# Batches 0 and 1 by head pair with a TensorE table for ALiBi and mask, later q and k transposed by DMA, and a fixed order on SyncE and GpSimd

## The chip, the cores and the metric

One core of one Trainium2 chip. The metric is the device time of one execution in microseconds (us); a kernel is given by the median of its runs. On one core an execution is called fast or slow by its distance from the fastest of the same kernel (over 1.5% is slow). A ratio between two kernels is the mean time of the fast runs of one over that of the other of the same rounds on the same chip, with a 95% interval, so it is not quite the ratio of the medians quoted beside it.

## The reference

```python
# q, k, v: (8 batches, 8 heads, 576, 64) fp32
scores = (q @ k.T) / sqrt(64)
mask   = (rel >= 0) & (rel < 128)              # rel = query - key: causal window of 128
scores = where(mask, scores - slope[h] * |rel|, -1e9)
attn   = softmax(scores) @ v
x      = heads joined: (4608 tokens, 512)
h      = x @ w_in                               # 512 -> 2048
out    = (h * sigmoid(beta * h)) @ w_out        # 2048 -> 512
```

## The kernel before

Per batch: 128-row blocks of q, k, v are loaded by SyncE (256 B rows, eight heads side by side), cast to bf16 by GpSimd, and q, k transposed by TensorE. Scores of one head pair fill a PSUM tile of two banks; four exponentials per tile carry the ALiBi bias, a multiply applies the mask. Tokens go through the two MLP layers in nine groups of 512. A "quad" is four 512-column matmuls: one hidden-layer tile (`HS`), or a quarter of an output tile (`OS`). While group g's hidden layer is computed, group g-1's output quads and the next tokens' attention are woven in. The order of TensorE's instructions is fixed by the program, the order of the other engines is chosen when it is built. Names in the profiles: `tps` is a PSUM tile of transposed q, k and `qkT` its copy in SBUF; `sps` (later `SS`, `OO`) holds scores, `pt` their exponentials, "PV" is the product of `pt` with v; `XT` is the transposed attention output that the MLP reads; `hps`, `sig` and `gT` are a hidden-layer tile, its tanh and the product of the two; `osb` is an output tile on its way to memory.

```python
    psum_h = ...tile_pool(name="psum_h", bufs=2, PSUM)
    psum_o = ...tile_pool(name="psum_o", bufs=2, PSUM)     # output tiles: two separate tiles of one bank
    psum_s = ...tile_pool(name="psum_s", bufs=1, PSUM)
    psum_t = ...tile_pool(name="psum_t", bufs=2, PSUM)
    # ... cut ...
    def T(b, sb):                                          # q, k of one 128-row block
        tps = psum_t.tile([P, 2, NP, P], BF16, name="tps", tag="t")
        for i in range(2):
            for p in range(NP):
                nc.tensor.transpose(out=tps[:, i, p, :], in_=src[:, i, 2*p:2*p+2, :]..., identity=ident[:])
        nc.vector.tensor_copy(out=QK[b % 2][:, :, :, P*sb : P*sb+rows], in_=tps[:, :, :, 0:rows])
    # ... cut ...
    def OS(g, i, n):
        if n == 0:
            opss[g, i] = psum_o.tile([P, DM], F32, name="ops", tag="ops")
        # ... four matmuls; after the fourth quad ScalarE copies the tile out (osb) and SyncE stores it
```

The softmax here doesn't subtract the row's maximum and nothing guards it: scores larger than these inputs give would overflow.

## Time and profile before

| | before |
|---|---|
| median | 374.81 us |
| first hidden-layer matmul | 42.44 us |
| TensorE busy | 338.5 us (90% of the span) |
| VectorE, ScalarE, GpSimd busy | 224.2, 214.4, 84.4 us |

Two rows of the page's slices, each digit the tenths of one fortieth of the span: TensorE's busy share and its granted clock.

```profile
PE   2367687788999999999999999999999999999995
PEclk9999999899999999999999999999999999999999
```

TensorE is short of work for the first quarter and full after it. In the list of groups (busy us, mean ns of one; then idle time before them and what ended it) two lines matter for what follows: the copy of transposed q and k into place, and the output matmuls.

```profile
L176 DVE COPY qkT<-tps 128x1024 bf16<-128x1024 bf16 x32 | 22.1, 690 | 19.6 <-PE tps L171 19.5
...
L283 PE MATMUL ops<-W,gT 128*128 128x512 bf16 x576 | 144.9, 379 | 0.0
```

The copy of 1024 columns takes 690 ns, and the 576 output matmuls never wait for anything.

### The profile page before, as it was taken

How to read it: one execution, taken by the hardware profiler on the slowest of the kernel's cores; microseconds unless marked ns; L12 is line 12 of the kernel's file. 1: busy time of each engine (PE TensorE's matmuls, PEld its weight loads, DVE VectorE, ACT ScalarE, POOL GpSimd, SP SyncE). 2: the span in 40 equal slices, each digit the busy share in tenths (PEclk: the TensorE clock that was granted, in tenths of full speed). 3: DMA queues.
4: the chain of work that ended last, by engine and by line, in shares of the span. 5: the costliest groups of instructions: out<-in, count | busy, mean ns of one | idle time of the engine just before them, and what ended most of it. 6: DMA issues, size and time to landing. Idle time of an engine off the chain costs nothing.

```text
span 374.6 us, 6713 instructions
## 1 busy us (share of the span) xinstructions
PE 338.5 (90%) x2529; PEld 172.7 (46%) x2529; DVE 224.2 (60%) x473; ACT 214.4 (57%) x437; POOL 84.4 (23%) x151
## 2 busy tenths in 40 slices
PE   2367687788999999999999999999999999999995
PEld 1145334434454455445454545454545445544442
DVE  3266467777665677665666776776767755533400
ACT  1453359375745875585846694668566854445421
POOL 7570703453122213112033303320100000000000
PEclk9999999899999999999999999999999999999999
DMA  9999999999297898954138440000000010001012
GB/s 166 209 206 202 193 195 214 192 216 180 76 214 159 159 186 170 205 126 107 50 96 187 109 104 31 28 30 29 30 28 30 30 57 29 29 29 58 28 56 86
DMA packets 121985, 42.40 MB, mean 113 GB/s; under 512 B 113232, under 2 KB 117344, under 8 KB 121952
## 3 DMA queue, kind: packets, MB, share of 16 engines
q1 hardware_dynamic: 117728, 37.77, 47.9%
q0 software_dynamic: 4224, 4.19, 6.7%
q8 instruction: 20, 0.33, 0.4%
q14 instruction: 13, 0.11, 0.1%
HBM read 36.71 MB, written 9.44 MB: 123 GB/s over the span
## 4 chain that ended last, share of the span: by engine, by line
PE 80%; DMA 6%; DVE 4%; ACT 4%; SPq 4%; issue 1%; POOL 0%; ACTq 0%
PE ops L283 34%; PE hps L267 32%; PE sps L197 4%; DMA fst<-in_k_dram 4%; PE tps L171 4%; SPq L83 4%; ACT pt L207 3%; PE xt L249 2%; PE pv L233 2%; DVE gT L273 2%; PE pv L229 2%; DMA fst<-in_v_dram 1%; ACT sig L272 1%; DVE pt L211 1%; DVE qkT L176 1%
## 5 line engine op out<-in xcount | busy, mean ns | idle before, releaser
L272 ACT ACTIVATE sig<-hps,beta_h 128x512 bf16<-128x512 f32 x144 | 99.5, 692 | 98.4 <-PE hps L267 87.4
L267 PE MATMUL hps<-XT,W 128*128 128x512 bf16 x576 | 150.7, 385 | 3.6 <-DVE gT L273 3.0
L283 PE MATMUL ops<-W,gT 128*128 128x512 bf16 x576 | 144.9, 379 | 0.0
L273 DVE SCALAR_TENSOR_TENSOR gT<-sig,hps 128x512 bf16<-128x512 bf16 x144 | 98.3, 683 | 53.0 <-ACT sig L272 52.4
L207 ACT ACTIVATE pt<-sps,bias 128x256 bf16<-128x256 f32 (+2 forms) x256 | 100.4, 480 | 34.9 <-PE sps L197 34.6
L267 PEld LDWEIGHTS <-W 128*128 128x128 bf16 x576 | 51.1, 98 | 56.5 <-issue 10.9
L283 PEld LDWEIGHTS <-gT 128*128 128x128 bf16 x576 | 51.3, 98 | 52.2 <-issue 1.7
L211 DVE TENSOR_TENSOR pt<-pt,mask 128x1024 bf16<-128x1024 bf16 x64 | 46.1, 720 | 21.2 <-ACT pt L207 20.0
L96 POOL CAST bst<-fst 128x512 bf16<-128x512 f32 (+1 forms) x40 | 24.6, 615 | 108.8 <-issue 78.7
L197 PE MATMUL sps<-qkT 64*128 64x256 bf16 (+2 forms) x320 | 28.3, 271 | 14.1 <-ACT pt L207 13.1
L104 POOL CAST vs<-fst 128x512 bf16<-128x512 f32 (+1 forms) x40 | 26.1, 659 | 65.0 <-PE pv L233 38.1
L176 DVE COPY qkT<-tps 128x1024 bf16<-128x1024 bf16 (+1 forms) x40 | 25.5, 637 | 21.5 <-PE tps L171 21.3
L171 PE MATMUL tps<-ident,bst 128*128 128x128 bf16 x320 | 28.8, 240 | 7.8 <-POOL bst L96 4.3
L239 DVE TENSOR_TENSOR xn<-pv,zs 128x256 bf16<-128x256 f32 (+1 forms) x80 | 33.7, 422 | 2.6
L289 ACT ACTIVATE osb<-ops 128x512 f32<-128x512 f32 x36 | 21.6, 601 | 20.8 <-PE ops L283 20.8
L233 PE MATMUL pv<-vs,pt 128*128 128x65 bf16 x320 | 31.0, 200 | 2.5 <-DVE xn L239 1.5
L171 PEld LDWEIGHTS <-bst 128*128 128x128 bf16 x320 | 23.5, 107 | 17.3 <-POOL bst L96 4.9
L197 PEld LDWEIGHTS <-qkT 64*128 64x128 bf16 x320 | 12.4, 97 | 38.2 <-issue 35.1
L233 PEld LDWEIGHTS <-pt 128*128 128x128 bf16 x320 | 23.6, 102 | 13.7 <-issue 1.8
L97 POOL CAST bst<-fst 128x512 bf16<-128x512 f32 (+1 forms) x40 | 25.3, 634 | 9.3 <-DMA fst<-in_k_dram 9.2
L229 PE MATMUL pv<-vs,pt 128*128 128x65 bf16 x256 | 25.8, 200 | 1.8 <-DVE qkT L176 1.2
L229 PEld LDWEIGHTS <-pt 128*128 128x128 bf16 x256 | 21.3, 102 | 8.3 <-DVE xn L239 1.3
(26 smaller groups left out, 74.3 us busy)
## 6 DMA issues: line engine op xcount, KB each, us to landing
out_dram<-osb SPq DMA_DIRECT2D x36, 256.0 KB, 2.0
fst<-in_q_dram SPq DMA_DIRECT2D x32, 256.0 KB, 4.8
fst<-in_k_dram SPq DMA_DIRECT2D x32, 256.0 KB, 4.8
fst<-in_v_dram SPq DMA_DIRECT2D x32, 256.0 KB, 5.0
W<-in_moe_w_in_dram POOLq DMA_DIRECT2D x4, 512.0 KB, 11.5
W<-in_moe_w_out_dram POOLq DMA_DIRECT2D x4, 512.0 KB, 12.6
fst<-in_q_dram SPq DMA_DIRECT2D x8, 128.0 KB, 4.2
fst<-in_k_dram SPq DMA_DIRECT2D x8, 128.0 KB, 4.2
```

The lines of the kernel that those rows point to most:

```text
L171: nc.tensor.transpose(out=tps[:, i, p, :], in_=src[:, i, 2 * p : 2 * p + 2, :].rearrange("r h d -> r (h d)"), identity=ident[:],)
L176: nc.vector.tensor_copy(out=QK[b % 2][:, :, :, P * sb : P * sb + rows], in_=tps[:, :, :, 0:rows])
L197: nc.tensor.matmul(o, lhsT=qk[64 * e : 64 * e + 64, 1, p, P * kb : P * kb + P], rhs=qk[64 * e : 64 * e + 64, 0, p, P * kb : P * kb + nq], ...
L207: nc.scalar.activation(out=pt[:, e, cols], in_=sps[:, e, cols], func=ACTF.Exp, scale=qscale, bias=bias[:, half, h : h + 1],)
L211: nc.vector.tensor_tensor(out=pt[:], in0=pt[:], in1=masks[m][:], op=ALU.mult)
L229: nc.tensor.matmul(pv[:, hl, 0 : D + 1], lhsT=weights(b, qb - 1, h, 1), rhs=vs[:, qb - 1, h, 0 : D + 1], start=True, stop=False,)
L233: nc.tensor.matmul(pv[:, hl, 0 : D + 1], lhsT=weights(b, qb, h, 0), rhs=vs[:, qb, h, 0 : D + 1], start=qb == 0, stop=True,)
L239: nc.vector.tensor_tensor(out=xn[0:nq, 4 * g : 4 * g + 4, :], in0=pv[0:nq, :, 0:D], in1=zs[0:nq].broadcast_to([nq, 4, D]), op=ALU.mult,)
L267: nc.tensor.matmul(hps[:], lhsT=W1[:, c, bass.ts(j, P)], rhs=XT[:, c, c0 : c0 + TOKG], start=(c == 0), stop=(c == NDM - 1),)
L272: nc.scalar.activation(out=sig[:], in_=hps[:], func=ACTF.Tanh, scale=beta_h[:, j : j + 1])
L273: nc.vector.scalar_tensor_tensor(out=gts[g][:, j, :], in0=sig[:], scalar=1.0, in1=hps[:], op0=ALU.add, op1=ALU.mult)
L283: nc.tensor.matmul(ops_[:], lhsT=gT[:, j, i * P : i * P + P], rhs=W2[:, j, :], start=(j == 0), stop=(j == NFF - 1),)
```

## The change

The intent: start the MLP sooner. For batches 0 and 1, q and k come one head pair at a time with four tokens, 1 KB, in one row per partition; TensorE first writes a table of ALiBi and mask into the score tile and adds the scores to it, so that one exponential per tile is enough. For batches 2 to 7, transposing DMAs take the q and k transposes off TensorE. SyncE's and GpSimd's order is now written out, and output stores go to GpSimd. The core of the diff:

```diff
+    def get_pair(what, b, p):                       # 4 tokens of one head = 1 KB in a row
+        return nc.sync.dma_start(out=f[:],
+            in_=src[b, 2*p : 2*p+2, 0:FULL, :].rearrange("h (r c) d -> r h (c d)", c=4))
+    def TP(b, p):
+        ... 8 x nc.tensor.transpose(out=tps[:, i, c], in_=src[:, i, c], identity=ident[:])
+        nc.vector.tensor_copy(
+            out=QK[b % 2][:, :, p, 0:FULL].rearrange("d i (r c) -> d i c r", c=4), in_=tps[:])
+    SS = psum_c.tile([P, 2, 512], F32, name="SS")
+    OO = psum_c.tile([P, 2, 512], F32, name="OO")
-    psum_o = ...tile_pool(name="psum_o", bufs=2, PSUM)
-    psum_s = ...tile_pool(name="psum_s", bufs=1, PSUM)
+    def SP_(b, vis, p):
+        sps = SS if vis == "A" else OO
+        ... two table matmuls (384 or 512 columns, start=True), then the scores on top (start=False)
+        nc.scalar.activation(out=pt[:, :, 0:w], in_=sps[:, :, 0:w], func=ACTF.Exp, scale=qscale)
+    def DT(b, sb):                                  # batches 2 to 7
+        nc.sync.dma_start(out=QK[b % 2][...], in_=src[...], transpose=True)
     def OS(g, i, n):
-        if n == 0:
-            opss[g, i] = psum_o.tile([P, DM], F32, name="ops", tag="ops")
-        ops_ = opss[g, i]
+        ops_ = OO[:, i % 2, :]
+    def constants_late():
+        ... 16 x nc.vector.tensor_copy(out=tablet[:, e, a, p], in_=table[:, 2*p+e, a, 0:64]), 5 memsets
+    with tc.manual_schedule(engines={ENG.PE, ENG.SP, ENG.Pool}):
+        ... batch 0, then hidden layer of group 0 with batch 1 woven in
+        # group 1: 8 hidden quads, then hidden and output quads in turn
+        # groups 2 to 8: two hidden quads to one output quad of the group before, then 8 of their own
 # ... cut: tails of 64 rows, constants, the old order ...
```

From the last group's first hidden-layer quad on, 40 quads remain instead of 48.

## The prediction

> **What bounds the kernel now.** I read the page first (busy shares, slices), then the busy time of each engine in three stretches, then the chain of waits, then TensorE's timeline in a full stretch. The stretches cut the kernel in three; the columns are length, then busy time and instructions of TensorE (PE), its weight loads, VectorE, ScalarE and GpSimd, then the granted clock, the DMA share and GB/s:
>
> ```profile
> 0.00:42.40 42.40, 21.71 (x197) 14.73 (x198) 20.64 (x64) 14.82 (x36) 23.25 (x52) 1.00 1.17 197
> 42.40:95.00 52.60, 41.00 (x323) 21.09 (x322) 36.84 (x74) 33.35 (x71) 22.75 (x37) 0.97 1.13 197
> 95.00:371.50 276.50, 275.80 (x2012) 136.86 (x2010) 166.74 (x336) 166.22 (x331) 38.39 (x64) 1.00 0.35 85
> ```
>
> From 95 us to the end TensorE never rests; there only less TensorE work helps. Before 95 us the DMA engines are full (share above 1) at 197 GB/s and TensorE is short of work. The chain of waits (start, length, what) says what the first MLP matmul waits for:
>
> ```profile
> 22.39 16.48 DMA fst<-in_k_dram
> 38.87 0.05 issue
> 38.92 0.62 POOL bst L97
> 39.55 0.05 issue
> 39.59 0.62 PE tps L171 x4
> 40.22 0.02 issue
> 40.24 0.70 DVE qkT L176
> 40.94 0.04 issue
> 40.98 0.40 PE sps L197 x2
> 41.38 0.56 PE xt L249 x4
> 41.93 0.02 issue
> 41.96 0.44 DVE XT L254
> 42.40 0.04 issue
> 42.44 1.88 PE hps L267 x4
> ```
>
> A k block (of batch 1, whose transposes TensorE meets in its queue before the last transposes of group 0) takes 16.48 us to land among W1 and the other loads; the MLP starts at 42.44 us. And TensorE where it is full; a start minus the next start is the true cost, since durations overlap:
>
> ```profile
> 128.32 1.03 PE L267 MATMUL hps<-XT,W 128*128 128x512 bf16 x4
> 129.19 0.61 PE L171 MATMUL tps<-ident,bst 128*128 128x128 bf16 x8
> 129.63 1.03 PE L283 MATMUL ops<-W,gT 128*128 128x512 bf16 x4
> 130.50 0.29 PE L233 MATMUL pv<-vs,pt 128*128 128x65 bf16 x4
> 130.63 1.02 PE L267 MATMUL hps<-XT,W 128*128 128x512 bf16 x4
> ```
>
> So four MLP matmuls cost 0.87 us (128.32 to 129.19; 0.864 in the mean), eight q/k transposes 0.44 (to 129.63), four PV matmuls 0.13. In the same way of reading, the four score matmuls of a pair took 0.32 (121.26 to 121.58), eight PV matmuls 0.24 (122.46 to 122.70), four output transposes 0.22 (124.86 to 125.08).
>
> **What the Trainium skill says.**
> 1. "TensorE: Matmul & The Clock Gate", Back-to-back issue gap: warm, about N/2.4 + 2.5 ns. The trace agrees: 216 ns at N = 512 (0.864/4) and 55 ns at N = 128 (0.44/8). I price the new 384- and 512-column table matmuls so.
> 2. "DMA: Bandwidth & Descriptors", Why small descriptors are slow: a fixed cost per packet, so 256 B rows waste the engines. The trace agrees in kind: 110,000-odd packets below 512 B, and full engines at only 197 GB/s.
> 3. The same page, Latency and other measured facts: 261 GB/s for one transposing DMA. Against it "VectorE: DVE Perf Modes", The three transpose paths: 1309 ns for one 128x128 block. No transposing DMA is in this trace; this is my largest unknown.
> 4. "SBUF — State Buffer", Door 1 trap: DMAs issued by GpSimd can starve for descriptors while VectorE holds the shared port. The output stores go there. In this trace the four W1 DMAs from GpSimd issue in 3.14 us and nothing shows the trap.
>
> **The change, part by part.**
> *TensorE work, before.* MLP 288 quads x 0.864 = 248.8. Transposes of q, k: 40 x 0.44 = 17.6. Scores: 64 x about 0.32 = 20.7. PV: 8 batches x (0.26 + 8 x 0.24) = 17.4. Output transposes 40 x 0.22 = 8.8. Sum 313 us. About 7 of it is done before 42.4 (batch 0), so 306 remain for the 329 us from 42.4 to 371.5: 23 us of idle and friction, some 12 of it visible before 95 (52.6 minus 41.0). Then 3 us of drain to 374.6.
> *Removed from TensorE.* q, k of batches 2 to 7: 6 x 5 x 0.44 = 13.2 us, all in the full stretch. VectorE loses 30 copies of about 0.69 (the qkT copy), which binds nothing.
> *Added to TensorE.* Table matmuls: per pair 2 x 384 and 2 x 512 columns = 0.32 + 0.43 us, x 8 pairs = 6.0, and the tail tables 0.9. Score matmuls of batches 0, 1 stay about as they were. New sum about 307.5 us, so the steady gain is only about 6.
> *Removed from ScalarE and VectorE, batches 0 and 1.* Four exponentials per tile (1.57 us a tile in the timeline) become one. The three sizes 192, 256, 320 take 430, 478, 532 ns in the group list, so 0.80 ns a column on 277 ns: 768 columns 0.89 us, 1024 columns 1.09. Batch 0 goes from 8 x 1.57 = 12.6 to 4 x 1.98 = 7.9, and the eight 0.69 us mask multiplies go. Besides, two score buffers alternate, where one buffer gave a cycle of 2.26 us (starts 14.83, 17.09, 19.36 of the score matmuls).
> *Loads.* Now one 256 KB block is issued every 1.19 us (SyncE 5.55, 6.74). Packets: queue 1 spent 47.9% of 16 x 374.6 us on 117,728 packets, 24 ns each at 321 B; queue 0 6.7% on 4,224 of 2 KB read, 95 ns each. Between the two a 1 KB packet is about 53 ns, so 256 KB is 256 x 53/16 = 0.85 us; estimate 0.8. Batch 0 is eight of these and four v blocks at 1.19: 11.2 us in all, and the order no longer puts batch 1 before group 0.
> *The new start.* First block lands near 4, then q, k of pairs 0, 1 by 6.1, v0, v1 by 8.5, pair 2 by 10.1, pair 3 by 11.7, the last v by 14. Per pair: two GpSimd casts 1.2, transposes 0.6, copy 0.7, scores 0.4, then exponentials 2.0. Pair 3's k is cast by 12.7, in QK by 14.1, its exponentials end near 16.5; PV, normalisation and transposes bring the first MLP matmul to 17 to 20 us, if W1's first quarter (issued near 11, 3.1 us of engine time at 95 ns a packet) has landed, which competes with the last loads. I take 19, plus 2 for what I have not seen: 21 us against 42.4.
> *From there.* Batch 0 now costs about 10 us of TensorE ahead of the MLP, so 297.5 remain. Friction: group 0 waits for batch 1, which is gated behind W1's second quarter (lands near 21): its pairs 2 and 3 are in near 35 us, v near 38. I put 4 us of TensorE idle there, 3 in group 1 (batch 2's score tiles at 2.26 us a turn within some 19 us), 8 in the steady groups, 3 of drain. 21 + 297.5 + 4 + 3 + 8 + 3 = 336.5 us.
>
> **The rivals.**
> (a) *The transposing DMA is slow.* A group of 512 tokens costs TensorE about 33 us, so a batch about 37: one 128-row block must be loaded, cast and transposed each 7.4 us. At 261 GB/s a block (256 KB) is 1.0 us and all is hidden. If its eight 128x128 blocks took 1.31 us each one after the other it is 10.5 us, 4.5 blocks a batch = 47 us: six batches 283 us after a start near 60, so 345 to 360 us. Since the loads of the next block stand behind the transposition in SyncE's fixed order, it could be worse. For it: nothing in the trace; against it: the DMA share is only 0.35 after 95 us. I give it 1 in 8.
> (b) *The start gives its gain back.* DMA engines stay the bound until W2 has landed: 3 MB of batch 0, 4 of W1, 3.8 of batch 1 and tails, 4 of W2 is about 15 MB, or 50 us at 300 GB/s; then batch 2 in 256 B rows, 18 us more. If each step slips, groups 0 and 1 hold 15 us more idle than I allow: 350 us. For it: W1's quarters took 7 to 16 us to land in this trace. 1 in 5.
> (c) *ScalarE binds in the steady groups.* The new order puts two hidden-layer quads to one output quad, so 16 tanh (0.69 us) and about two thirds of a group's exponentials (7.3 us) fall into 24.5 us: 19.5 us busy, 80%, in order, with two PSUM buffers between. Now it is 60% (166/276). Each score tile can delay a tanh by 1.57 us. That would be 1 to 2 us a group, 7 groups: 345 us. 1 in 4.
> (d) *Stores on GpSimd hold up the casts.* In its fixed order a store waits for its output tile, and casts stand behind it. The casts are a batch ahead, so I expect nothing.
>
> **Range and chances.** Without rivals 330 to 337; with (b) or (c) 345 to 350; with (a) 345 to 360 and, rarely, no gain. I predict 338 us, 8 in 10 between 327 and 352. Faster by over 2% means below 367.3, 29 us above my sum: 0.95. Within 2%: 0.03. Slower: 0.02.
>
> **What would show it right or wrong.** The first hidden-layer matmul near 21 us (17 to 25); after it stands the sum of the rest. TensorE's q/k transposes fall from 320 to 80 (two batches), with 0.44 us per eight unchanged. The exponentials of 768 and 1024 columns at 0.9 and 1.1 us. Pair loads at 0.8 us a block, DMA at about 300 GB/s in the first 12 us. A transposing DMA of 256 KB landing in less than 7 us, and no TensorE wait on it. TensorE busy over 97% from about 65 us on; gaps there behind tanh would be (c), gaps before score matmuls (a). I am wrong if the MLP starts after 28 us, if SyncE is seen held by transpositions while loads wait, or if idle after the MLP start sums to over 30 us.

## The result, and the profile after

The changed kernel took 388.06 us (386.62 to 388.25, 4 runs) where the kernel before took 375.32 in the same rounds: ratio 1.0345, interval 1.0305 to 1.0385. It is 3.4% slower, and 50 us above the prediction.

The same two rows of the page show that the start is still poor, and that the clock is near half in parts of it:

```profile
PE   3676868699879999989999989999999899999985
PEclk9765799969989999999999999999999999999999
```

TensorE's clock record has four half-speed stretches: 15.4 to 22.2, 25.6 to 42.7, 76.8 to 83.6 and 107.5 to 111.0 us, 34 us in all; the kernel before has one of 3.4 us. In the 3.4 us before each of the four, TensorE was busy for only 37 to 51% of the time.

By stretch, cut at the first hidden-layer matmul of groups 0, 1 and 2 and at the end of TensorE's work (columns as in the prediction):

```profile
0.00:31.80 31.80, 18.18 (x158) 9.85 (x159) 19.31 (x51) 8.82 (x10) 18.83 (x47) 0.80 1.02 219
31.80:77.70 45.90, 32.97 (x275) 15.57 (x275) 31.99 (x71) 19.01 (x25) 17.65 (x29) 0.87 1.03 184
77.70:132.10 54.40, 48.36 (x323) 21.58 (x323) 25.35 (x51) 30.17 (x62) 15.15 (x25) 0.91 0.72 131
132.10:382.40 250.30, 238.66 (x1605) 111.59 (x1603) 137.40 (x282) 148.26 (x294) 51.31 (x89) 1.00 0.50 106
```

TensorE idles 13 to 14 us in each of the first two stretches, and even in the last, where the kernel before was busy for 251.60 of 251.60 us (from 119.2 us on), it idles 11.6. The chain of work that ended last (start, length, what) names the start's cost:

```profile
6.07 2.44 DVE qkT L233
...
11.57 2.44 DVE qkT L233
...
16.46 2.43 DVE qkT L233
...
22.28 2.43 DVE qkT L233
...
32.30 2.70 DVE tablet L123 x16
```

Four copies of transposed q, k stand one after the other in the chain, at 2.43 us each. Then 16 small copies of the tail table hold VectorE for 2.7 us, just when the first group's last XT copy is due. The group list has the same copy, and the output matmuls:

```profile
L457 PE MATMUL OO<-W,gT 128*128 128x512 bf16 x576 | 143.7, 381 | 11.5 <-ACT osb L463 11.4
...
L233 DVE COPY qkT<-tps 128x1024 bf16<-128x1024 bf16 x8 | 19.5, 2434 | 6.5 <-PE tps L232 6.5
```

The copy has the same 128x1024 bf16 in and out as the old 690 ns one; only its order of writing is new: every fourth bf16 of the destination, 8 bytes apart. And output matmuls, which waited for nothing before, now wait 11.4 us for ScalarE's copy of an output tile. The timeline of the last tiles (start, length, engine, line) shows which copy. After the change:

```profile
365.23 0.60 ACT L463 ACTIVATE osb<-OO 128x512 f32<-128x512 f32 x1 [0.17 <-PE OO L457]
365.88 3.61 PE L457 MATMUL OO<-W,gT 128*128 128x512 bf16 x16 [0.69 <-ACT osb L463]
...
369.53 0.60 ACT L463 ACTIVATE osb<-OO 128x512 f32<-128x512 f32 x1 [3.70 <-PE OO L457]
370.18 3.61 PE L457 MATMUL OO<-W,gT 128*128 128x512 bf16 x16 [0.69 <-ACT osb L463]
```

And before:

```profile
357.69 13.11 PE L283 MATMUL ops<-W,gT 128*128 128x512 bf16 x60
...
360.48 0.60 ACT L289 ACTIVATE osb<-ops 128x512 f32<-128x512 f32 x1 [2.86 <-PE ops L283]
...
363.93 0.60 ACT L289 ACTIVATE osb<-ops 128x512 f32<-128x512 f32 x1 [2.85 <-PE ops L283]
```

Before, a tile begins while the one ahead of it is copied out: one tile per 3.45 us. After, each tile starts 0.05 us after the end of the copy of the tile just ahead, although that one lies in the other bank: one per 4.30 us. The two halves of `OO` are one tile to whatever places the waits.

Waits of TensorE in the second stretch (31.8 to 77.7 us), then from 132 us on (us in total, times, longest):

```profile
PE SS L275 <- DVE qkT L233: 2.7, 2, 2.2
PE hps L436 <- DVE gT L444: 2.7, 4, 1.1
PE hps L436 <- DVE XT L316: 2.0, 1, 2.0
...
```

```profile
PE OO L457 <- ACT osb L463: 9.4, 14, 1.2
```

And the part that I had been most in doubt of, the transposing DMAs (count, median us from issue to landing):

```profile
qkT<-bst SPq DMA_TRANSPOSE x30, 3.8
```

No wait of TensorE in this kernel ends with one of them.

The account below sets the profiled run (388.25 us) beside my sum. TensorE's work is counted from the matmul records at full-clock costs (0.216 us for 512 columns, 0.055 for a transpose, 0.030 for a PV matmul, tables and scores by their columns, so an estimate of a few us); idle time is the length of a stretch minus that work, so it holds half-clock time too. Priced instead along the line through 55 ns at 128 columns and 216 ns at 512 (which gives 251.3 us for the 251.6 us in which the kernel before was always busy), the work is 302.7 us and the idle time of the steady groups 16.8 and 4.9 us in place of 19.4 and 7.5: the column is good to some 3 us. The last column is the mended kernel of the experiments below (profiled run 356.84 us).

| | predicted | after | mended (best1) |
|---|---|---|---|
| until the first hidden-layer matmul | 21 | 31.8 | 23.4 |
| TensorE work from there | 297.5 | 299.7 | 299.7 |
| idle in group 0 | 4 | 19.8 | 11.3 |
| idle in group 1 | 3 | 11.8 | 8.3 |
| idle in the steady groups and the last | 8 | 19.4 | 7.5 |
| drain and rest of the time | 3 | 5.9 | 6.7 |
| sum | 336.5 | 388.3 | 356.9 |

### The profile page after: what moved, and what is told of

Same layout as the page of the kernel before. It is cut to its first block, busy times and chain, and to the rows that moved or that the text cites. A ratio compares the mean times of both kernels' runs of the same rounds, so it can differ in the third digit from the quotient of the medians.

```text
span 386.5 us, 6289 instructions
## 1 busy us (share of the span) xinstructions
PE 338.2 (87%) x2357; PEld 158.6 (41%) x2357; DVE 214.1 (55%) x454; ACT 206.9 (54%) x392; POOL 102.9 (27%) x188
## 3 DMA queue, kind: packets, MB, share of 16 engines
q0 software_dynamic: 6944, 13.11, 13.2%
## 4 chain that ended last, share of the span: by engine, by line
PE 71%; DVE 14%; ACT 11%; issue 3%; DMA 1%; POOL 0%; ACTq 0%
PE OO L457 30%; PE hps L436 28%; ACT pt L374 6%; DVE qkT L233 5%; PE SS L364 3%; DVE gT L444 3%; ACT osb L463 3%; DVE pt L378 2%; ACT sig L443 2%; PE xt L414 1%; PE pv L403 1%; PE pv L399 1%; PE tps L232 1%; PE pv L304 1%; DVE xnp L289 1%
## 5 line engine op out<-in xcount | busy, mean ns | idle before, releaser
L457 PE MATMUL OO<-W,gT 128*128 128x512 bf16 x576 | 143.7, 381 | 11.5 <-ACT osb L463 11.4
L374 ACT ACTIVATE pt<-SS,bias 128x256 bf16<-128x256 f32 (+1 forms) x192 | 75.0, 477 | 21.2 <-PE SS L364 21.2
L436 PEld LDWEIGHTS <-W 128*128 128x128 bf16 x576 | 53.5, 100 | 70.2 <-issue 20.9
L470 POOL DMA_DIRECT2D out_dram<-osb x34 | 18.4, 542 | 214.1 <-ACT osb L463 214.1
L463 ACT ACTIVATE osb<-OO 128x512 f32<-128x512 f32 x36 | 21.7, 604 | 47.1 <-PE OO L457 45.5
L288 DVE RECIPROCAL zs<-pv 128x4 f32<-128x4 f32 (+1 forms) x80 | 13.8, 176 | 31.2 <-PE pv L403 24.5
L196 POOL CAST bst<-fst 128x512 bf16<-128x512 f32 (+1 forms) x32 | 21.2, 661 | 30.2 <-PE tps L232 16.9
L420 DVE COPY XT<-xt 128x512 bf16<-128x512 bf16 (+1 forms) x32 | 12.3, 385 | 19.6 <-PE xt L414 19.3
L233 DVE COPY qkT<-tps 128x1024 bf16<-128x1024 bf16 x8 | 19.5, 2434 | 6.5 <-PE tps L232 6.5
L364 PE MATMUL SS<-qkT 64*128 64x256 bf16 (+2 forms) x240 | 19.4, 256 | 3.3 <-ACT pt L374 3.3
L403 PE MATMUL pv<-vs,pt 128*128 128x65 bf16 x240 | 20.6, 193 | 0.0
L403 PEld LDWEIGHTS <-pt 128*128 128x128 bf16 x240 | 16.1, 97 | 6.7
L399 PE MATMUL pv<-vs,pt 128*128 128x65 bf16 x192 | 17.4, 193 | 0.0
```

Source lines behind the costliest of these rows:

```text
L233: nc.vector.tensor_copy(out=QK[b % 2][:, :, p, 0:FULL].rearrange("d i (r c) -> d i c r", c=4), in_=tps[:])
L364: nc.tensor.matmul(o, lhsT=qk[64 * e : 64 * e + 64, 1, p, P * kb : P * kb + P], rhs=qk[64 * e : 64 * e + 64, 0, p, P * kb : P * kb + nq], ...
L374: nc.scalar.activation(out=pt[:, e, cols], in_=sps[:, e, cols], func=ACTF.Exp, scale=qscale, bias=bias[:, half, h : h + 1],)
L403: nc.tensor.matmul(pv[:, hl, 0 : D + 1], lhsT=weights(b, qb, h, 0), rhs=vs[:, qb, h, 0 : D + 1], start=qb == 0, stop=True,)
L436: nc.tensor.matmul(hps[:], lhsT=W1[:, c, bass.ts(j, P)], rhs=XT[:, c, c0 : c0 + TOKG], start=(c == 0), stop=(c == NDM - 1),)
L457: nc.tensor.matmul(ops_, lhsT=gT[:, j, i * P : i * P + P], rhs=W2[:, j, :], start=(j == 0), stop=(j == NFF - 1),)
```

## The experiments

All kernels gave correct results; every ratio is against the kernel before. My theory after the result: (1) the strided copy and the shared output tile are two faults of the form, not of the idea, and with the late table copies they hold most of the loss; (2) the DMA transposes do what they should. The rivals: the idea itself is at fault (too little TensorE work left to weave, or the DMA transposes hold SyncE), or the lower clock is the cause.

### oo2: the output accumulator as two tiles

```diff
-    OO = psum_c.tile([P, 2, 512], F32, name="OO")
+    OO = [psum_c.tile([P, 512], F32, name=f"OO{i}") for i in range(2)]
-        ops_ = OO[:, i % 2, :]
+        ops_ = OO[i % 2][:]
     # in SP_, visit B: two exponentials of 512 columns instead of one of 1024
```

> The output accumulator OO becomes two one-bank tiles in place of one two-bank tile; the second exponential of a pair in batches 0 and 1 becomes two of 512 columns for it (about 0.35 us more, 8 times). Theory A: as one tile, each output tile waits for the ScalarE copy of the tile just before it, though that is in the other bank; the profile shows 17 such waits with about 0.85 us lost at each (last stage: 4.30 us per tile where the kernel before has 3.45). Then the lost TensorE time of groups 2 to 8 falls from about 19 us to under 6, the last four tiles run at 3.45 us, and the total falls by 12 to 18 us to 370 to 376. Rival: the waits are only where the slack of the two-to-one order (ScalarE, two hidden-layer buffers) shows, and it moves elsewhere: total falls by less than 5 us.

374.48 us, ratio 0.9981 (0.9892 to 1.0071): some 13 us less than after. The waits are gone:

```profile
L461 PE MATMUL OO<-W,gT 128*128 128x512 bf16 x554 | 138.0, 379 | 1.4 <-issue 0.5
```

(22 of the 576 records are missing here.) The last group, from its first tanh to the end of TensorE's work, fell from 37.0 to 33.6 us. One PSUM tile for two accumulators cost some 13 us by time. By the two profiled runs, 12.4 us apart, 10.0 us of it lie in groups 2 to 8, where TensorE's work ran at full clock in both; group 1 gave 3.4 us more, but it had 7.4 us of half clock before and 1.0 now, so a part of these is the clock's. (The second edit, two exponentials where there was one, adds eight exponentials at the start.)

### cpc and rows256: the strided copy

Two ways to be rid of the stride on the writing side. In cpc the copy writes in order and reads PSUM with the stride; the 1 KB rows stay.

```diff
-  out=QK[..].rearrange("d i (r c) -> d i c r", c=4), in_=tps[:]
+  out=QK[..].rearrange("d i (r c) -> d i r c", c=4), in_=tps[:].rearrange("d i c r -> d i r c")
```

> The copy of transposed q, k of batches 0 and 1 writes 512 contiguous columns and reads PSUM with the stride instead. Theory B (the 8-byte write stride makes the copy 2.43 us in place of the 0.69 us that I predicted): the copy falls to 0.7 to 1.2 us, the first hidden-layer matmul comes at 25 to 28 us in place of 31.8, and the total falls by 6 to 12 us. Rival (any stride costs it, on either side): the copy stays above 2 us and the time is the same within 1 us.

In rows256 the tokens keep their order in the load, so nothing is permuted, at the price of 256 B rows and two DMAs per block.

```diff
-  out=f[:], in_=src[b, 2*p : 2*p+2, 0:FULL, :].rearrange("h (r c) d -> r h (c d)", c=4)
+  for e in range(2):
+    out=f[:, e].rearrange("r (c d) -> r c d", d=D), in_=src[b, 2*p+e, 0:FULL, :].rearrange("(c r) d -> r c d", c=4)
-  out=QK[..].rearrange("d i (r c) -> d i c r", c=4)
+  out=QK[..].rearrange("d i (c r) -> d i c r", c=4)
```

> Undoes the 1 KB rows alone: q, k of a head pair come in 256 B rows, two DMAs a block, and the copy needs no stride. Theory B: copies 0.69 us, blocks 1.19 us in place of about 0.8; the chain of batch 0 loses 4 x 1.7 us of copies and gets at most 3 us of loads back, so the first hidden-layer matmul comes at 26 to 28 us and the total falls by 6 to 12 us (376 to 382). Rival (the rows are worth their stride, since loads bind the start): first hidden-layer matmul at 31 us or later, total the same or longer.

cpc: 378.77 us, ratio 1.0114 (1.0047 to 1.0181). rows256: 373.62, ratio 0.9966 (0.9914 to 1.0017). The copy in cpc, then in rows256:

```profile
L233 DVE COPY qkT<-tps 128x1024 bf16<-128x1024 bf16 x8 | 9.7, 1218 | 4.3 <-PE tps L232 4.2
```

```profile
L233 DVE COPY qkT<-tps 128x1024 bf16<-128x1024 bf16 x8 | 5.5, 688 | 6.8 <-PE tps L232 6.8
```

So one and the same 128x1024 bf16 copy takes 0.69 us in order on both sides, 1.22 with a stride on the PSUM side (256 bytes, since there the four tokens lie 128 columns apart), and 2.43 with an 8-byte stride on the SBUF side. Side and length of the stride changed together, so which of them makes the difference between these two is not shown. The Trainium skill, "Advanced Engine Details and Errata", 2x-1p Requirements, has the first step: VectorE's fast mode wants a unit step in the innermost dimension. The 0.53 us between 0.69 and 1.22 agree with the loss of such a mode; for the further factor of two the page gives no figure.

In rows256 the first hidden-layer matmul on record comes at 23.64 us against 31.76 (in cpc at 27.22; one record of these first matmuls is missing in both, which can be 0.2 to 0.4 us). Four copies in a row are 4 x (2.43 - 0.69) = 7.0 of these 8.1 us, and in cpc 4 x (2.43 - 1.22) = 4.8 of 4.5. The whole gain, 14 us, is more than I had expected: batch 1's four copies go too, and the profile has 6.8 us at half clock before 50 us instead of 24. How much of the start's gain belongs to the clock, no run here separates. In group 1 it can be read, since none of cpc, rows256 and late changes the program there: from its first tanh to the next group's it takes 53.5 us in the changed kernel and in late, with 7.4 and 7.5 us at half clock, and 51.5 in cpc and rows256, with none. So 7.4 us of half clock cost 2.0 us there.

### late: the table copies off the path

```diff
     constants_late():  make_identity(identf)           # stays
+    constants_dve():   the 16 tablet copies and 5 memsets, called right after SP_(0, "B", 0)
```

> The sixteen table copies and the memsets (4.2 us of VectorE from 32.2 us on) move to the first gap of VectorE, after the first pair's scores. Theory C: they hold up the copy of the last transposed output of batch 0, for which the hidden layer waits 2 us, and the first products behind it: total falls by 3 to 5 us. Rival (TensorE runs at half clock there and the MLP is bound by its own products): less than 1.5 us.

384.59 us, ratio 1.0259 (1.0205 to 1.0313): 3.5 us less than after. A real but small part.

### best1: the three together

oo2, rows256 and late in one kernel.

> The changed kernel with the three mends together: two one-bank output tiles, 256 B rows without the strided copy, table copies moved to VectorE's first gap. If the three causes are separate, their measured gains (13, 14 and 3.5 us) add up: 388 minus about 31 gives 355 to 361 us. If they hide one another (two of them lie in the same start and group 0) the sum is smaller: 362 to 368.

358.05 us, ratio 0.9542 (0.949 to 0.9593). The three gains (13.6, 14.4 and 3.5 us) add up to 31.5; measured are 30. So within the noise the gains add up, and the idea, without these faults, is 4.6% faster than the kernel before. The rival that the idea itself is at fault falls. The clock is no rival of the same size: best1 has 6.8 us at half clock where the changed kernel had 34, and time at half clock can cost at most half of its length, 14 us for the 27 saved (at the rate of group 1, an estimate, 7).

### best1_1kb: are the 1 KB rows worth their permutation?

best1 with the 1 KB rows and cpc's copy in place of rows256.

> best1 with 1 KB rows kept and the copy reading PSUM with the stride (1.22 us a copy) in place of 256 B rows. In the single runs that copy was worth 9 us and the 256 B rows 14 us, so 2 to 6 us longer than best1. Rival: with the other waits gone the faster loads win, equal or shorter than best1.

361.5 us, ratio 0.964 (0.9586 to 0.9695), 3.5 us slower than best1 in the same rounds. The DMA engines did deliver faster with 1 KB rows (261 GB/s from 2 to 14 us in the changed kernel, 223 in best1), but the permutation costs more than that gives back.

### best1_nodt and before_dt: the DMA transposes alone

best1_nodt takes them out of best1; before_dt puts them, and nothing else, into the kernel before.

```diff
  # best1_nodt, in DT
- nc.sync.dma_start(out=QK[..], in_=src[..], transpose=True)
+ 8 x nc.tensor.transpose(...) into a PSUM tile, then one nc.vector.tensor_copy into QK
  # and four of batch 2's first jobs instead of five stand ahead of group 1, so that no transposition does
  # before_dt, at the end of load_qk; T returns at once for b >= 2
+ if b >= 2: nc.sync.dma_start(out=QK[..], in_=t[..], transpose=True)
```

> The same with q, k of batches 2 to 7 transposed by TensorE again. Theory D (transposing DMAs are hidden and TensorE is the bound there): 30 times eight transposes of 0.44 us come back, 10 to 13 us longer than best1 (365 to 373). Rival (TensorE has idle time in those groups which absorbs them, or the DMAs held something up): within 4 us of best1.

> The kernel before with one part of the change alone: q, k of batches 2 to 7 transposed by DMA right after their casts. Theory D: TensorE loses 13 us of transposes in the stretch where it never rests, so 362 to 367 us. Rival (SyncE's queue, where loads and stores now stand behind transposes that wait for casts, takes it back): 370 us or longer.

best1_nodt: 373.22 us, ratio 0.9941 (0.9903 to 0.9979), 15 us slower than best1. Between the two profiled runs, 4.4 us of the difference lie before the first tanh, where the edit changes nothing but where best1_nodt has 9.1 us of half clock (of a stretch of 13.7) and best1 none; the groups hold the other 13, close to the 13.2 us of TensorE work that the prediction counted. before_dt: 368.14, ratio 0.9794 (0.9752 to 0.9836), only 7.5 us faster, which is between the two expectations. Its groups 1 to 7 are 11.7 us shorter in sum (tanh to tanh), but group 0 is 4.3 us longer, and the waits of TensorE say why:

```profile
PE sps L204 <- DMA qkT<-bst: 7.5, 2, 4.4
```

In the old order of loads, batch 2's first transposing DMAs come too late for its scores, 7.5 us in two waits near 70 us, and 10.2 us at half clock begin at 70.0 us (3.4 in the kernel before). The transposition itself is no slower than in the changed kernel: 3.3 us to landing in the median and 5.3 at most, against 3.8 and 6.6. The longer wait is for the third one. It was issued only at 72.44 us, after the cast of its k block at 71.80; in the kernel before, the same cast began at 66.49. SyncE's queue now holds transpositions, which wait for casts, in front of loads; that this delays the loads is the likely reason and was not tested apart. In the changed kernel, where the order of SyncE and GpSimd is written out, no such wait is left. That the two halves of the change belong together is thus supported, not shown: no run has the changed order alone in the kernel before.

### best1_gi, best1_gf, best1_gif: where the mended kernel still loses

The account leaves 11.3 and 8.3 us idle in groups 0 and 1 of best1, against 4 and 3 predicted. Its waits of TensorE in group 0 (23.4 to 60.9 us; 8.8 us in all, of which the largest is shown), then group 1 (60.9 to 111.7):

```profile
PE hps L442 <- DVE gT L450: 3.2, 4, 1.3
```

```profile
PE SS L370 <- ACT pt L380: 3.0, 3, 1.9
```

The first is the phase of hidden-layer quads only, in which two PSUM tiles go through matmuls, tanh and multiply in turn:

```profile
30.01 1.89 PE L442 MATMUL hps<-XT,W 128*128 128x512 bf16 x8 [0.64 <-DVE gT L450]
32.53 1.89 PE L442 MATMUL hps<-XT,W 128*128 128x512 bf16 x8 [0.63 <-DVE gT L450]
```

Two quads take 2.52 us there, 1.26 each instead of 0.864. Group 1 begins with eight such quads, and ends with batch 2's score tiles in a crowd, each waiting for the exponentials of the one ahead. Two edits, alone and together:

```diff
  # gi: hidden and output quads in turn from the start of group 1
- items = h[:8] ... then h[8+n], o[n] in turn
+ items = h[n], o[n] in turn for n in range(16)
  # gf: batch 2's score tiles begin after 14 items of group 1
- spread([...], 22, len(items) - 2, need[2])
+ spread([...], 14, len(items) - 2, need[2])
```

> The mended version, with one more edit: in group 1 hidden-layer and output quads alternate from the first item on, instead of eight hidden-layer quads in a row first. Theory A (hidden-layer quads in a row are bound by latency: 1.26 us each instead of 0.864, because two PSUM tiles alternate with tanh and the multiply): the eight quads at the start of group 1 lose 8 x 0.4 = 3.2 us, and the alternation saves 2 to 4 us: 354 to 356 against 358. Theory B (group 1 loses its 8 us to the score tiles of batch 2 with one score buffer, late in the group): no change, within 1 us of 358, since the score tiles stay as crowded as they were.

> The mended version, with one more edit: the score tiles of batch 2 begin after 14 of group 1's items instead of after 22, so that they are spread over more output quads. Theory B (the crowded score tiles cost group 1 its time): 2 to 5 us are saved, 353 to 356. Theory A (hidden-layer quads in a row cost it): within 1 us of 358, or slower if batch 2's data is not in yet when the first score tile is met (the transposing DMA would then end a wait of TensorE for the first time).

> Both edits. If A and B both hold, the savings add up: 350 to 354. If group 1 loses its time to something else (data that comes late), nothing is saved: 357 to 359, and the trace names the data.

Medians 356.92, 356.17 and 355.54 us; ratios 0.9484 (0.9427 to 0.954), 0.9491 (0.9435 to 0.9548) and 0.948 (0.9425 to 0.9535). All three medians lie just above what was expected (354 to 356, 353 to 356 and 350 to 354). By time this is inconclusive: all lie a little below best1's 0.9542, and all intervals overlap its interval. By the profiles there is something: group 1 (tanh to tanh) takes 50.6 us in best1, 48.4 in gf and 46.3 in gif (gi's profiled run is not used). But the half clock within the group falls in the same order, 6.3, 2.9 and 0 us. best1_1kb, which has best1's order of group 1 and no half clock there, takes 49.2. So at full clock the two edits together shorten the group by 2.9 us, 1.4 of the 4.3 go with the clock, and what each edit does alone is not shown. The waits agree with a small effect: in group 1 of best1 only 0.8 us of TensorE's waits are for `gT`, and the waits for exponentials fall from 3.0 to 2.3 us in gf and gif. The whole gains some 2 us at most. gif is the fastest kernel, 5% faster than the kernel before. The profiled run of gif even started its groups 4 us later than that of gf (30.2 against 26.2), with 13.7 us of half clock from 21 us on. Among gif's own four runs the time falls with the mean granted clock, from 357.42 at 0.980 to 354.06 at 1.000; among oo2's it does not. No experiment here held the clock itself fixed, so its share of the whole stays open.

## Why the prediction was wrong

**The step that failed first** is in "Per pair: two casts 1.2, transposes 0.6, copy 0.7, scores 0.4, then exponentials 2.0". The copy took 2.43 us, not 0.7. I took its duration from a row of the same shape and type and did not read its access pattern, which the diff shows plainly. Four of them in a row are 7.0 of the 10.8 us by which the MLP started later than 21 us; at 31.8 us it also lay beyond the 28 that I had named as a sign of being wrong, as did the idle time after it, 51 us against 30. With an ordered copy (best1) it started at 23.4, inside the range that I gave for this view (17 to 25).

**The second** is the term "8 in the steady groups", which measured 19.4. I asked there whether ScalarE was too busy (rival c), and did not ask what the two halves of one PSUM tile do to the waits. The diff shows this one too: two pool buffers became one tile of two banks. With two tiles the term is 7.5 (4.9 in the other pricing), so the 8 was about right for the kernel as it was meant, and leaves no room for rival (c) in its own sense (tanh late behind exponentials).

**The third** is "4 us of TensorE idle there, 3 in group 1". Measured: 19.8 and 11.8. In group 0, waits for batch 1's strided copies and for the late table copies are among the largest shown (the qkT and XT lines above), and 11.8 us of it ran at half clock; the mended kernel still has 11.3 and 8.3. I priced quads at 0.864 us wherever they stand; in a row without other work they cost 1.26. That is shown for the phases of group 0; in group 1 the two edits found 2.9 us at full clock, and the rest of the term is not settled.

**Not in the sum at all:** the granted clock. 34 us at half clock, in stretches that follow a starved TensorE, against 3.4 before. It goes with the faults (fewer such stretches when they are mended) but comes back in single profiled runs of mended kernels. In group 1 it cost 2.0 us for 7.4 at half clock; at that rate the 34 us are some 9, an estimate, and they can't be more than 17.

**Small slips.** The new TensorE work is 313.3 - 13.2 + 6.9 = 307.0 us, not 307.5; 367.3 is 29 us above the 338, and 31 above the sum. The 3 us of drain were read from a span, and the time of a run is 1.7 us longer than its span (388.25 against 386.5). The passage that the prediction names "Door 1 trap" stands on the page "SBUF — State Buffer" under "SBUF: two separate sides"; no run here shows the trap.

**What was right.** TensorE's work from the MLP's start: 297.5 predicted, 299.7 counted. The transposing DMA: 3.8 us to landing (6.6 at most) against my bound of 7, no wait on it, and 13.2 us of TensorE work gone, which best1_nodt and best1 show as 13 to 15 us. The exponentials of 768 and 1024 columns took 0.81 and 1.02 us against 0.89 and 1.09. Stores on GpSimd hold nothing up: they land in 2.3 us, and after the start no wait of TensorE ends with a cast. The DMA rate of about 300 GB/s in the first 12 us was too high: 224. Rival (b), that the start gives its gain back, holds in part: best1's MLP starts 19 us sooner than before's, and the kernel is 17.6 us faster with 13 to 15 us of that owed to the DMA transposes.

So of the 50 us between prediction and result, 30 were two faults of form and one misplaced block of copies, and undoing them shows it; of the other 20 (best1's 356.8 against the sum of 336.5), the account gives 12.6 to idle time in groups 0 and 1, 3.7 to the drain and the rest of the time, 2.4 to the start and 2.2 to TensorE's work. The idle time is part latency of hidden-layer quads in a row and crowded score tiles, part clock, of which only the first two were touched by experiments, and their effect is small.

## What to carry to other kernels

A duration taken from a row of the old profile holds for the same access pattern, not for the same shape: read the strides of every copy that a change adds, and put a permutation where it costs least (here the load, even at 256 B rows). Two accumulators that alternate should be two tiles; as one tile, each waited for the other here. And an asynchronous transposition is only worth the TensorE time that it frees if it is issued early enough (7.5 us in the old order of loads, 13 to 15 in the new one), so try it together with an order that fits it.

## What the Trainium skill lacked or had wrong

- "Advanced Engine Details and Errata", 2x-1p Requirements: right about the unit step, as far as 0.69 against 1.22 us goes. For a strided SBUF destination the page has a warning in words (SBUF Cachelines) and no figure. A 128x1024 bf16 copy from PSUM that writes with an 8-byte stride took 2.43 us, twice the one that reads PSUM with a stride.
- "DMA: Bandwidth & Descriptors", Latency and other measured facts, and "VectorE: DVE Perf Modes", The three transpose paths: from 261 GB/s and from 1309 ns for one 128x128 block I got 1.0 and 10.5 us for a DMA of eight blocks (estimates), since neither page says how the blocks of one DMA overlap. The transposing DMAs here landed 3.8 us after issue (median of 30 with other DMAs under way, 3.1 to 6.6), 0.48 us a block for eight.
- "TensorE: Matmul & The Clock Gate", HAM oscillation: it warns of idle gaps over about 3.4 us. Here the clock was halved for 34 us in stretches between 15 and 111 us, with no gap between matmuls over 2.2 us after the first one had started. The page's next part, on short idle times between groups of matmuls, is nearer to this; no run here tests it.
- No page that I read says that two halves of one PSUM tile are waited on as one. It cost 10 to 13 us here.
